# Two key blocks' scores handled as one 2048-wide unit in a decode kernel of attention and a gated mixer

## The chip, the cores and the metric

One core of one Trainium2 chip. The time is device microseconds of one execution; lower is better. Executions of the kernel before agree within 0.2%.

## The reference, cut to what matters

One token attends to 65536 cached keys; 32 query heads share 4 key/value groups. A second branch is a small gated mixer, and a sigmoid gate mixes both.

```python
q = (x @ wq) ...                       # 32 heads of 128
scores = einsum('bhqd,bhkd->bhqk', q, k) * Dh ** -0.5
p = softmax(scores)                    # over 65536 keys
a = einsum('bhqk,bhkd->bhqd', p, v) ... @ wo
b = mixer(x, w_in, w_sp, b_sp, w_out)
out = g * a + (1 - g) * b              # g = sigmoid(sum(x * gate_w))
```

Everything is bf16. The caches are 134 MB of the 162 MB that have to be read, and each byte is used once. Inputs are small (0.05 times normal), so the scores are close to zero.

## The kernel before

The key cache is cut into 16 blocks of 16384 keys ("keys 0" to "keys 15", four per group), 4 MB each, and the value cache likewise. SyncE issues the loads in one fixed order into a ring of five 4 MB slots. Slots 0 to 2 take keys, slots 3 and 4 take values, and most loads are of two blocks, 8 MB. A load is issued only when every block that its slots held has been used up. That is a wait on the last reader: the fourth transpose of a key block on VectorE, or the last value matmul on TensorE.

```python
def k_piece(n, p):                     # a quarter of key block n
    ...
    P("DVE", ... transpose 128x2048 f32 of the quarter into ktb(i) ...)   # two buffers
    if p == 3:
        done(("k", n))                 # the ring slot is free: the next load may be issued
    def f(e): ...                      # 8 score matmuls into sc_ps(n), the half n % 2 of PSUM
    P("PE", f, r=["qpad", ("kt", i % NKT)], w=[KSC(n)])

def score_piece(n):                    # 1024 wide: PSUM -> SBUF, with the running maximum
    P("DVE", lambda e: e.tensor_scalar(scs(n), sc_ps(n), 0.0, None, op0=ALU.add, op1=ALU.max,
                                       accum_out=maxc[:, n:n + 1]), w=[("sc", n % NSC), ("mx", n), KSC(n)])

def exp_piece(n):  ...                 # ScalarE, 1024 wide
def pt_piece(n):   ...                 # VectorE transpose of the probabilities, 1024 wide
def pv_piece(n):   ...                 # TensorE: value matmuls of block n, then done(("v", n))

def k_step(n, evac=None, gmax=None, pts=(), own=False, mid=None):
    for p in range(4):
        k_piece(n, p)
        if p == 0 and evac is not None:
            score_piece(evac)          # evac is n - 1: the other half of PSUM
            ...
```

The load order of the main loop, which the argument needs:

```python
for i in range(6):
    a = 2 * i + 4
    if i % 3 == 2:
        load_k(a, 2)                   # 4 MB each
        load_k(a + 1, 0)
    else:
        load_k2(a, (1, 0)[i % 3])      # 8 MB in one load, needs two free slots
    load_v2(2 * i, VB)
```

## Time and profile before

| | before |
|---|---|
| time, median of 3 (range) | 382.55 us (382.42 to 382.6) |
| bytes read | 162 MB, 425 GB/s over the span |
| load queue, share of 16 engines | 98.6% |
| VectorE / TensorE / ScalarE busy | 55% / 59% / 7% |

From the page of the kernel before: engine shares, then the rows of the span in 40 slices (a digit is the busy share in tenths, PEclk the granted TensorE clock), the load queue, and the chain that ended last.

```profile
PE 223.8 (59%) x1375; PEld 54.6 (14%) x785; DVE 210.4 (55%) x229; ACT 25.4 (7%) x39; POOL 1.8 (0%) x9
DVE  4112596879079606966991069735984990242020
PEclk9997599896869995999896969995899995969766
DMA  9999999999999999999999999999989999999995
q1 hardware_dynamic: 4192, 162.01, 98.6%
DMA 63%; DVE 21%; PE 13%; SPq 1%; issue 0%; ACTq 0%; DVEq 0%
```

The DMA row is 9 nearly everywhere, so the memory stream is the limit and VectorE, with many low digits, is not. But VectorE has 21% of the chain. That is because the chain passes through the transposes that free a ring slot.

The groups of VectorE and ScalarE that the change touches (line, engine, operation, shapes, count; busy us, mean ns of one; idle time of the engine before them, and what ended it):

```profile
L484 DVE STREAM_TRANSPOSE arena<-arena 128x2048 f32<-128x2048 f32 x64 | 145.0, 2290 | 72.0 <-DMA arena<-in_A_k_cache_dram 62.0
L501 DVE TENSOR_SCALAR_CACHE_REDUCE arena<-scp 128x1024 f32<-128x1024 f32 x16 | 19.1, 1191 | 17.6 <-PE scp L248 17.6
L522 DVE STREAM_TRANSPOSE arena<-arena 128x1024 bf16<-128x1024 bf16 x16 | 19.4, 1214 | 8.9 <-PE obt L248 6.4
```

What the change touches is L501 and L522, 38 us in 32 instructions; the 145 us of key transposes stay.

VectorE in order of time in the step of keys 4 (start, duration, engine, line, what):

```profile
106.96 2.31 DVE L484 STREAM_TRANSPOSE arena<-arena 128x2048 f32<-128x2048 f32 x1 [8.70 <-DMA arena<-in_A_k_cache_dram]
109.19 1.19 DVE L501 TENSOR_SCALAR_CACHE_REDUCE arena<-scp 128x1024 f32<-128x1024 f32 x1
...
110.76 2.30 DVE L484 STREAM_TRANSPOSE arena<-arena 128x2048 f32<-128x2048 f32 x1
...
113.23 2.30 DVE L484 STREAM_TRANSPOSE arena<-arena 128x2048 f32<-128x2048 f32 x1
115.46 1.20 DVE L522 STREAM_TRANSPOSE arena<-arena 128x1024 bf16<-128x1024 bf16 x1
116.59 2.27 DVE L484 STREAM_TRANSPOSE arena<-arena 128x2048 f32<-128x2048 f32 x1
```

And the queue of SyncE: the load that this step lets go.

```profile
118.88 0.33 SPq L373 DMA_DIRECT2D arena<-in_A_k_cache_dram  x1
```

The evacuation (L501) follows the first key transpose with no gap. The fourth transpose ends at 118.86, and the load of keys 6,7 is issued at 118.88.

### The profile page before, as it was taken

What the parts mean: (1) busy time and instruction counts of PE and PEld (TensorE: products, weight loads), DVE (VectorE), ACT (ScalarE), POOL (GpSimd) and SP (SyncE); (2) the same over time, 40 slices, a digit from 0 to 9 for tenths busy, and PEclk for the clock granted to TensorE, in tenths of its full rate; (3) what the DMA queues carried; (4) which work ended last, traced back from release to release, by engine and by line L of the source; (5) the groups of instructions that cost most, each with busy time, mean ns of one, the idle gap of its engine ahead of it and who ended that gap; (6) DMA issues with size and microseconds to landing.
All of it is one profiled execution on the core that took longest, in us unless ns stands there. A gap on an engine that the chain in (4) does not pass through costs nothing.

```text
span 381.5 us, 2501 instructions
## 1 busy us (share of the span) xinstructions
PE 223.8 (59%) x1375; PEld 54.6 (14%) x785; DVE 210.4 (55%) x229; ACT 25.4 (7%) x39; POOL 1.8 (0%) x9
## 2 busy tenths in 40 slices
PE   0060479458456844786756636862779643869373
PEld 0010012011011200121111101210112101212031
DVE  4112596879079606966991069735984990242020
ACT  1000000010212000100210001000300100121000
POOL 1000000000000000000000000000000000000000
PEclk9997599896869995999896969995899995969766
DMA  9999999999999999999999999999989999999995
GB/s 440 433 426 405 440 386 436 437 485 443 428 433 405 405 435 440 440 419 436 443 428 440 440 440 440 435 440 434 440 378 414 460 440 433 433 411 429 417 424 212
DMA packets 4238, 162.16 MB, mean 425 GB/s; under 512 B 508, under 2 KB 516, under 8 KB 772
## 3 DMA queue, kind: packets, MB, share of 16 engines
q1 hardware_dynamic: 4192, 162.01, 98.6%
q8 instruction: 8, 0.13, 0.1%
q14 instruction: 2, 0.02, 0.0%
q10 hardware_dynamic: 36, 0.00, 0.0%
HBM read 162.01 MB, written 0.00 MB: 425 GB/s over the span
## 4 chain that ended last, share of the span: by engine, by line
DMA 63%; DVE 21%; PE 13%; SPq 1%; issue 0%; ACTq 0%; DVEq 0%
DMA arena<-in_A_k_cache_dram 40%; DVE arena L484 16%; DMA arena<-in_A_v_cache_dram 10%; DMA arena<-in_A_wo_dram 8%; DMA arena<-in_B_b_sp_dram 5%; PE obt L246 3%; PE obt L248 3%; PE scp L246 3%; PE scp L248 3%; DVE arena L522 2%; DVE arena L501 1%; SPq L373 0%; ACTq L272 0%; SPq L350 0%; PE scp L427 0%
## 5 line engine op out<-in xcount | busy, mean ns | idle before, releaser
L484 DVE STREAM_TRANSPOSE arena<-arena 128x2048 f32<-128x2048 f32 x64 | 145.0, 2290 | 72.0 <-DMA arena<-in_A_k_cache_dram 62.0
L246 PE MATMUL scp<-arena 128*128 128x512 bf16 x256 | 106.3, 415 | 97.5 <-DVE arena L484 94.2
L248 PE MATMUL scp<-arena 128*128 128x512 bf16 x256 | 104.9, 410 | 0.0
L246 PE MATMUL obt<-arena 128*64 128x512 bf16 (+2 forms) x334 | 63.8, 423 | 22.0 <-DMA arena<-in_A_v_cache_dram 22.0
L248 PE MATMUL obt<-arena 128*64 128x512 bf16 (+2 forms) x334 | 63.1, 418 | 0.0
L246 PEld LDWEIGHTS scp<-arena 128*128 128x128 bf16 x256 | 26.2, 103 | 198.7 <-DVE arena L484 124.6
L517 ACT ACTIVATE arena<-arena 128x1024 bf16<-128x1024 f32 x16 | 18.4, 1151 | 226.8 <-DVE arena L522 115.7
L246 PEld LDWEIGHTS obt<-arena 128*64 128x64 bf16 (+1 forms) x334 | 18.6, 114 | 77.6 <-issue 58.8
L501 DVE TENSOR_SCALAR_CACHE_REDUCE arena<-scp 128x1024 f32<-128x1024 f32 x16 | 19.1, 1191 | 17.6 <-PE scp L248 17.6
L522 DVE STREAM_TRANSPOSE arena<-arena 128x1024 bf16<-128x1024 bf16 x16 | 19.4, 1214 | 8.9 <-PE obt L248 6.4
L547 DVE RECIPROCAL arena<-mbt 128x1 f32<-128x1 f32 x4 | 0.7, 168 | 26.3 <-PE mbt L543 26.3
L731 PE MATMUL fbt<-arena 128*1 128x256 bf16 x128 | 6.4, 364 | 4.0 <-DMA arena<-in_A_wo_dram 3.9
L415 PE MATMUL scp<-arena 8*128 8x1 bf16 x8 | 0.6, 197 | 11.1 <-DVE arena L410 11.1
L420 PE MATMUL mbt<-arena 1*128 1x2 bf16 x1 | 0.2, 158 | 10.1 <-DMA arena<-in_B_b_sp_dram 10.1
L737 DVE CAST arena<-fbt 97x256 bf16<-97x256 f32 x1 | 0.4, 425 | 9.7 <-PE fbt L731 9.7
L422 DVE COPY arena<-mbt 128x2 f32<-128x2 f32 x1 | 0.2, 159 | 10.1 <-PE mbt L420 10.1
L562 PE MATMUL mbt<-arena 128*128 128x128 bf16 x16 | 2.0, 262 | 4.7 <-DVE arena L557 4.7
L731 PEld LDWEIGHTS fbt<-arena 128*1 128x1 bf16 x128 | 3.4, 104 | 7.0 <-DMA arena<-in_A_wo_dram 3.0
L606 ACT ACTIVATE arena<-arena 128x28 f32<-128x28 f32 x1 | 0.2, 228 | 56.7 <-DVE arena L605 56.7
L472 DVE COPY arena<-arena 32x32 bf16<-32x32 bf16 x16 | 2.6, 164 | 2.2 <-PE scp L248 2.0
L449 DVE CAST arena<-obt 97x1024 bf16<-97x1024 f32 x1 | 1.2, 1225 | 4.7 <-PE obt L248 4.7
L568 DVE TENSOR_TENSOR arena<-mbt,arena 128x128 f32<-128x128 f32 x4 | 1.2, 292 | 4.4 <-PE mbt L562 4.4
(89 smaller groups left out, 51.0 us busy)
## 6 DMA issues: line engine op xcount, KB each, us to landing
arena<-in_A_k_cache_dram SPq DMA_DIRECT2D x6, 4096.0 KB, 33.5
arena<-in_A_v_cache_dram SPq DMA_DIRECT2D x2, 4096.0 KB, 23.8
arena<-in_B_w_in_dram SPq DMA_DIRECT2D x1, 7168.0 KB, 30.9
arena<-in_A_wo_dram SPq DMA_DIRECT2D x3, 2048.0 KB, 28.6
arena<-in_B_w_out_dram SPq DMA_DIRECT2D x1, 3584.0 KB, 20.7
arena<-in_A_wo_dram SPq DMA_DIRECT2D x1, 1280.0 KB, 30.9
arena<-in_A_wo_dram SPq DMA_DIRECT2D x1, 512.0 KB, 31.6
arena<-in_A_wo_dram SPq DMA_DIRECT2D x1, 256.0 KB, 31.1
```

The source lines that it names most:

```text
L246: return e.matmul(*a, **kw)
L248: one = e.matmul(*a, **kw).ins
L449: P("DVE", lambda e: e.tensor_copy(psb[0:97, :], ob[0:97, :]), w=["psb", "ob"])
L472: P("DVE", lambda e, pb=pb: e.tensor_copy(vw(qpad, 24 + 32 * pb, [[QP, 4], [1, 8]], 32 * pb, 32), vw(qall, 8 * g, [[32, 4], [1, 8]], 32 * ...
L484: P("DVE", lambda e: e.transpose(ktb(i).bitcast(F32), sl[:, 4096 * p:4096 * (p + 1)].bitcast(F32)), r=keys[4 * p:4 * p + 4], w=[("kt", i % ...
L501: P("DVE", lambda e: e.tensor_scalar(scs(n), sc_ps(n), 0.0, None, op0=ALU.add, op1=ALU.max, accum_out=maxc[:, n:n + 1]), w=[("sc", n % NSC ...
L517: P("ACT", lambda e: e.activation(psb, scs(n), ACTF.Exp, bias=gcol(n // NP, K_NB), scale=SCALE, accum_out=lp[:, n:n + 1]), r=[("sc", n % N ...
L522: P("DVE", lambda e: e.transpose(ptsb(n), psb), r=["psb"], w=[("ptsb", n % 2)])
L547: P("DVE", lambda e: e.reciprocal(gcol(g, K_RL), mb[:, 0:1]), w=[("rl", g), "mb"])
L562: ins = e.matmul(mb[:, 0:128], sel[:, 128 * c:128 * (c + 1)], osc[:, 128 * c:128 * (c + 1)], start=(c == 0), stop=(c == 3))
L568: P("DVE", lambda e: e.tensor_tensor(vw(ot, 0, [[8, 16], [1, 8]]), vw(mb, 0, [[8, 16], [1, 8]]), vw(mq, 0, [[1, 16], [0, 8]]), ALU.mult), ...
L731: ins = e.matmul(fb[32 * q:32 * q + 1, 0:QW], ovec[:, 8 * i + c:8 * i + c + 1], sl[:, o:o + QW], start=False, stop=(i == 3 and c == 7), ti ...
```

## The change

Intent: keep the work but halve the number of instructions on VectorE and ScalarE. The scores of two key blocks become one PSUM tile of 2048 columns, evacuated, exponentiated and transposed as one unit; the maximum and the normaliser use fewer small operations; small copies and memsets go to GpSimd. The diff, cut to its core:

```diff
-    scp = [nc.alloc_psum_tensor("scp%d" % i, [128, 1024], F32) for i in range(2)]
+    scp = nc.alloc_psum_tensor("scp", [128, 2048], F32)
...
     def q_piece(g):
         for pb in range(4):
-            P("DVE", lambda e, pb=pb: e.tensor_copy(vw(qpad, ...
+            P("POOL", lambda e, pb=pb: e.tensor_copy(vw(qpad, ...
...
-    def score_piece(n):
-        P("DVE", lambda e: e.tensor_scalar(scs(n), sc_ps(n), 0.0, None, op0=ALU.add, op1=ALU.max,
-                                           accum_out=maxc[:, n:n + 1]), w=[("sc", n % NSC), ("mx", n), KSC(n)])
+    def score_pair(j):
+        P("DVE", lambda e: e.tensor_scalar(scs(j), scp[:, :], 0.0, None, op0=ALU.add, op1=ALU.max,
+                                           accum_out=maxc[:, j:j + 1]),
+          w=[("sc", j % 2), ("mx", j), KSC(0), KSC(1)])
...
-    def k_step(n, evac=None, gmax=None, pts=(), own=False, mid=None):
+    def k_step(n, evac=None, gmax=None, pts=None, mid=None):
         for p in range(4):
             k_piece(n, p)
             if p == 0 and evac is not None:
-                score_piece(evac)
+                score_pair(evac)
...
-            if p == 2 and pts:
-                pt_piece(pts[0])
-                exp_piece(pts[1])
-            if p == 3 and pts:
-                pt_piece(pts[1])
...
+        if pts is not None:
+            pt_pair(pts)
...
-        k_step(a, evac=a - 1, gmax=(a - 1) // NP if a % NP == 0 else None, pts=(2 * i, 2 * i + 1))
+        k_step(a, evac=i + 1, gmax=i // 2 if i % 2 == 0 else None, pts=i)
```

Note the place of `score_pair(evac)`. Before, block n wrote one PSUM half while the evacuation read the other. Now the evacuation reads both halves, and it still stands after the first matmuls of block n. So it waits for them, and those matmuls have already started to overwrite the even block's scores.

More of the change, by code (lines that the diff above doesn't have):

```diff
@@ L166, in bass_gated_mix__gqa_block_cached__mixer_gmlp__decode_kernel @@
     NKT = 2
-    NSC = 5
+    NSC = 4
     QW = DO // 4
@@ L184, in bass_gated_mix__gqa_block_cached__mixer_gmlp__decode_kernel @@
     for name, n in [
-        ("RING", NSUB * SUB), ("KT", NKT * 4096), ("SC", NSC * 2048), ("PSB", 1024), ("PTSB", 2 * 1024),
+        ("RING", NSUB * SUB), ("KT", NKT * 4096), ("SC", NSC * 2048), ("PSB", 2 * 1024), ("PTSB", 2 * 1024),
         ("QPAD", 4 * QP), ("IDB", 128), ("BM", 256), ("SEL", 16 * 32),
         ("M16", 32), ("MQ", 32), ("XT", KC), ("WB", 2), ("WBB", 4), ("ONEB", 128),
-        ("MAXC", 2 * total), ("LP", 2 * total), ("COLS", 2 * 64), ("DM", 32), ("QALL", 128), ("OV", OC), ("MHALF", 4),
+        ("MAXC", 2 * total), ("LP", 2 * total), ("COLS", 2 * 64), ("DM", 64), ("ONES", 256), ("QALL", 128), ("OV", OC), ("MHALF", 4),
         ("YB", FC), ("OROW", QW),
@@ L204, in vw @@
                        ap=[[ps, np_]] + [list(d) for d in dims])
-    idb, bm, ones = ab("IDB", 128), af("BM", 128), af("SC", 128, 4 * 1024 + 896)
+    idb, bm, ones = ab("IDB", 128), af("BM", 128), af("ONES", 128)
     sel, m16, mq = ab("SEL", 512), af("M16", 16), af("MQ", 16)
@@ L212, in bass_gated_mix__gqa_block_cached__mixer_gmlp__decode_kernel @@
     yb, ovec, orow = ab("YB", FC), ab("OV", OC), ab("OROW", QW)
-    dm = af("DM", 16)
-    psb = ab("PSB", 1024)
+    dm = af("DM", 32)
+    psb, psb2 = ab("PSB", 1024), ab("PSB", 2048)
     osc, ot = ab("PSB", 512), af("PSB", 128, 256)
@@ L221, in gcol, with gcol2 @@
         return col(C_G4 + 12 * g + i)
+    def gcol2(g, i):
+        return colt[:, C_G4 + 12 * g + i:C_G4 + 12 * g + i + 2]
     (K_M, K_NB, K_MH, K_L, K_RL, K_F, K_FA, K_FB) = range(8)
     ktb = lambda i: ab("KT", 4096, (i % NKT) * 4096)
-    scs = lambda n: af("SC", 1024, (n % NSC) * 1024)
+    scs = lambda j: af("SC", 2048, (j % 2) * 2048)
     ptsb = lambda i: ab("PTSB", 1024, 1024 * (i % 2))
-    scp = [nc.alloc_psum_tensor("scp%d" % i, [128, 1024], F32) for i in range(2)]
+    ptsb2 = ab("PTSB", 2048)
+    scp = nc.alloc_psum_tensor("scp", [128, 2048], F32)
     obt = nc.alloc_psum_tensor("obt", [128, 1024], F32)
@@ L232, in bass_gated_mix__gqa_block_cached__mixer_gmlp__decode_kernel @@
     fbt = nc.alloc_psum_tensor("fbt", [128, 512], F32)
-    sc_ps = lambda n: scp[n % 2][:, :]
+    sc_ps = lambda n: scp[:, 1024 * (n % 2):1024 * (n % 2 + 1)]
     ob, mb, fb = obt[:, :], mbt[:, :], fbt[:, :]
-    tb = scp[1][:, 0:512]
+    tb = scp[:, 1024:1536]
     tbh = tb.bitcast(BF16)
@@ L249, in mm @@
         return e.add_instruction(dataclasses.replace(one, name=nc.get_next_instruction_name(), ldweights=False))
-    idf = af("SC", 128, 4 * 1024)
-    m8 = af("SC", 8, 4 * 1024 + 128)
-    m32 = af("SC", 32, 4 * 1024 + 136)
-    qT = ab("SC", 32, 4 * 2048 + 400)
+    idf = af("SC", 128, 0)
+    m8 = af("SC", 8, 128)
+    m32 = af("SC", 32, 136)
+    qT = ab("SC", 32, 400)
     P("POOL", lambda e: e.memset(idf, 0.0), w=["idf"])
@@ L261, in bass_gated_mix__gqa_block_cached__mixer_gmlp__decode_kernel @@
     P("POOL", lambda e: e.memset(orow, 0.0), w=["orow"])
-    P("DVE", lambda e: e.memset(ones, 1.0), w=["ones"])
-    P("DVE", lambda e: e.memset(oneb, 1.0), w=["oneb"])
+    P("POOL", lambda e: e.memset(ones, 1.0), w=["ones"])
+    P("POOL", lambda e: e.memset(oneb, 1.0), w=["oneb"])
     P("DVE", lambda e: e.memset(mb, 0.0), w=["mb"])
@@ L272, in f @@
                 return e.dma_start(dst, src)
-        P("ACT", f, w=[key], dma="l%s" % (key if isinstance(key, str) else key[1]))
+        P("ACT", f, w=[key], dma="l" + key)
     xrow, grow, prod = ab("SC", 512, 3 * 2048), ab("SC", 512, 2 * 2048), af("SC", 512, 1 * 1024)
     xm = ab("SC", 1024, 3 * 2048 + 512)
-    KX, KG, KP = ("sc", 3), ("sc", 2), ("sc", 1)
+    KX, KG, KP = "xr", "gr", "pr"
     small(xrow[0:8, 0:128], A_x[0, 0].rearrange("(i n) -> i n", i=8), KX)
@@ L390, in bass_gated_mix__gqa_block_cached__mixer_gmlp__decode_kernel @@
     P("DVE", lambda e: e.tensor_reduce(m16, vw(idf, 0, [[8, 16], [1, 8]]), AXX, ALU.add), r=["idf"], w=["m16"])
-    P("DVE", lambda e: e.tensor_copy(vw(bm, 0, [[8, 16], [1, 8]]), vw(m8, 0, [[0, 16], [1, 8]])), r=["m8"], w=["bm"])
+    P("POOL", lambda e: e.tensor_scalar(m16, m16, -SCALE, None, op0=ALU.mult), r=["m16"], w=["m16"])
+    P("POOL", lambda e: e.tensor_copy(vw(bm, 0, [[8, 16], [1, 8]]), vw(m8, 0, [[0, 16], [1, 8]])), r=["m8"], w=["bm"])
     P("DVE", lambda e: e.tensor_reduce(m32, vw(idf, 0, [[1, 32], [32, 4]]), AXX, ALU.add), r=["idf"], w=["m32"])
-    P("DVE", lambda e: e.tensor_copy(col(C_E4), m32[:, 0:1]), r=["m32"], w=["e4"])
-    P("DVE", lambda e: e.tensor_copy(vw(sel, 0, [[16, 32], [1, 16]]), vw(m32, 0, [[1, 32], [0, 16]])),
+    P("POOL", lambda e: e.tensor_copy(col(C_E4), m32[:, 0:1]), r=["m32"], w=["e4"])
+    P("POOL", lambda e: e.tensor_copy(vw(sel, 0, [[16, 32], [1, 16]]), vw(m32, 0, [[1, 32], [0, 16]])),
       r=["m32"], w=["sel"])
@@ L399, in bass_gated_mix__gqa_block_cached__mixer_gmlp__decode_kernel @@
       r=["idf"], w=["mhalf"])
-    sele = ab("SC", 512, 4 * 2048 + 512)
+    sele = ab("SC", 512, 512)
     KSE = "sele"
     for fe in range(4):
-        P("DVE", lambda e, fe=fe: e.tensor_copy(vw(sele, 128 * fe, [[32, 4], [1, 32]]),
+        P("POOL", lambda e, fe=fe: e.tensor_copy(vw(sele, 128 * fe, [[32, 4], [1, 32]]),
                                                 vw(idb, 64 * (fe // 2) + fe % 2, [[0, 4], [2, 32]])),
@@ L433, in bass_gated_mix__gqa_block_cached__mixer_gmlp__decode_kernel @@
       r=["g"], w=["omg"])
+    P("DVE", lambda e: e.tensor_scalar(mhalf, mhalf, col(C_G), None, op0=ALU.mult), r=["mhalf", "g"], w=["mhalf"])
     wqs, keys = use(("wq", 0))
@@ L471, in q_piece @@
         for pb in range(4):
-            P("DVE", lambda e, pb=pb: e.tensor_copy(vw(qpad, 24 + 32 * pb, [[QP, 4], [1, 8]], 32 * pb, 32),
+            P("POOL", lambda e, pb=pb: e.tensor_copy(vw(qpad, 24 + 32 * pb, [[QP, 4], [1, 8]], 32 * pb, 32),
                                                     vw(qall, 8 * g, [[32, 4], [1, 8]], 32 * pb, 32)),
@@ L504, in max_first @@
     def max_first(g):
-        P("DVE", lambda e: e.tensor_reduce(gcol(g, K_M), maxc[:, NP * g:NP * (g + 1)], AXX, ALU.max),
-          r=[("mx", NP * g + u) for u in range(NP)], w=[("m", g)])
-        P("DVE", lambda e: e.tensor_scalar(dm, m16, gcol(g, K_M), None, op0=ALU.mult), r=["m16", ("m", g)], w=["dm"])
-        P("PE", lambda e: e.matmul(mb[:, 0:16], bm, dm, start=True, stop=True), r=["bm", "dm"], w=["mb"])
+        P("DVE", lambda e: e.tensor_tensor(vw(dm, 0, [[16, 2], [1, 16]]), vw(m16, 0, [[0, 2], [1, 16]]),
+                                           vw(maxc, 2 * g, [[1, 2], [0, 16]]), ALU.mult),
+          r=["m16", ("mx", 2 * g), ("mx", 2 * g + 1)], w=["dm"])
@@ L511, in max_second @@
+        P("PE", lambda e: e.matmul(mb[:, 0:32], bm, dm, start=True, stop=True), r=["bm", "dm"], w=["mb"])
     def max_second(g):
-        P("DVE", lambda e: e.tensor_reduce(gcol(g, K_MH), mb[:, 0:16], AXX, ALU.max), w=[("mh", g), "mb"])
-        P("DVE", lambda e: e.tensor_scalar(gcol(g, K_NB), gcol(g, K_MH), -SCALE, None, op0=ALU.mult),
-          r=[("mh", g)], w=[("nb", g)])
-    def exp_piece(n):
-        P("ACT", lambda e: e.activation(psb, scs(n), ACTF.Exp, bias=gcol(n // NP, K_NB), scale=SCALE,
-                                        accum_out=lp[:, n:n + 1]),
-          r=[("sc", n % NSC), ("nb", n // NP)], w=["psb", ("lp", n)])
@@ L521, in pt_piece, with exp_pair, pt_pair @@
-    def pt_piece(n):
-        P("DVE", lambda e: e.transpose(ptsb(n), psb), r=["psb"], w=[("ptsb", n % 2)])
+        P("DVE", lambda e: e.tensor_reduce(gcol(g, K_NB), mb[:, 0:32], AXX, ALU.min), w=[("nb", g), "mb"])
+    def exp_pair(j):
+        P("ACT", lambda e: e.activation(psb2, scs(j), ACTF.Exp, bias=gcol(j // 2, K_NB), scale=SCALE,
+                                        accum_out=lp[:, j:j + 1]),
+          r=[("sc", j % 2), ("nb", j // 2)], w=["psb", ("lp", j)])
+    def pt_pair(j):
+        P("DVE", lambda e: e.transpose(ptsb2, psb2), r=["psb"], w=[("ptsb", 0), ("ptsb", 1)])
@@ L524, in pv_piece, with pt_half @@
+    def pt_half(n):
+        P("DVE", lambda e: e.transpose(ptsb(n), ab("PSB", 1024, 1024 * (n % 2))), r=["psb"], w=[("ptsb", n % 2)])
     def pv_piece(n):
@@ L540, in out_first, with f @@
     def out_first(g):
-        P("DVE", lambda e: e.tensor_reduce(gcol(g, K_L), lp[:, NP * g:NP * (g + 1)], AXX, ALU.add),
-          r=[("lp", NP * g + u) for u in range(NP)], w=[("l", g)])
-        P("PE", lambda e: e.matmul(mb[:, 0:1], bm, gcol(g, K_L), start=True, stop=True),
-          r=["bm", ("l", g)], w=["mb"])
+        def f(e):
+            for h in range(2):
+                ins = e.matmul(mb[:, 0:1], bm, lp[:, 2 * g + h:2 * g + h + 1], start=(h == 0), stop=(h == 1))
+            return ins
+        P("PE", f, r=["bm", ("lp", 2 * g), ("lp", 2 * g + 1)], w=["mb"])
     def out_second(g):
         P("DVE", lambda e: e.reciprocal(gcol(g, K_RL), mb[:, 0:1]), w=[("rl", g), "mb"])
-        P("DVE", lambda e: e.tensor_scalar(gcol(g, K_F), gcol(g, K_RL), col(C_G), None, op0=ALU.mult),
-          r=[("rl", g), "g"], w=[("f", g)])
-        for h, k in ((0, K_FA), (1, K_FB)):
-            P("DVE", lambda e, h=h, k=k: e.tensor_scalar(gcol(g, k), mhalf[:, h:h + 1], gcol(g, K_F), None, op0=ALU.mult),
-              r=[("f", g), "mhalf"], w=[("fh", g, h)])
+        P("DVE", lambda e: e.tensor_scalar(gcol2(g, K_FA), mhalf, gcol(g, K_RL), None, op0=ALU.mult),
+          r=[("rl", g), "mhalf"], w=[("fh", g)])
     def out_third(g):
         P("DVE", lambda e: e.tensor_scalar(osc, ob[:, 0:512], gcol(g, K_FA), None, op0=ALU.mult),
-          r=[("fh", g, 0)], w=["psb", "ob"])
+          r=[("fh", g)], w=["psb", "ob"])
         P("DVE", lambda e: e.scalar_tensor_tensor(osc, ob[:, 512:1024], gcol(g, K_FB), osc, op0=ALU.mult, op1=ALU.add),
-          r=[("fh", g, 1), "psb"], w=["psb", "ob"])
+          r=[("fh", g), "psb"], w=["psb", "ob"])
         def f(e):
@@ L591, in mixer_piece @@
         NZ = 2 * FB4
-        zr, zt = af("SC", NZ, 3 * 1024), af("SC", NZ, 4 * 1024)
-        KZR, KZT = ("sc", 3), ("sc", 4)
-        zw = lambda i: af("SC", 28, 3 * 1024 + 32 * i)
+        zr, zt = af("SC", NZ, 2 * 1024), af("SC", NZ, 3 * 1024)
+        KZR, KZT = ("sc", 1), "zt"
+        zw = lambda i: af("SC", 28, 2 * 1024 + 32 * i)
         zc = vw(zt, 0, [[32, 28]])
@@ L644, in wout_piece @@
         done(("wout", 0))
-        part = scs(4)
-        P("ACT", lambda e: e.activation(part[0:97, :], ob[0:97, :], ACTF.Copy), w=[("sc", 4), "ob"])
+        part = af("SC", 1024, 2 * 1024)
+        P("ACT", lambda e: e.activation(part[0:97, :], ob[0:97, :], ACTF.Copy), w=[("sc", 1), "ob"])
         def f(e):
@@ L652, in f @@
             return ins
-        P("PE", f, r=["e4", ("sc", 4)], w=["fb"])
-    def k_step(n, evac=None, gmax=None, pts=(), own=False, mid=None):
+        P("PE", f, r=["e4", ("sc", 1)], w=["fb"])
+    def k_step(n, evac=None, gmax=None, pts=None, mid=None):
         for p in range(4):
@@ L665, in k_step @@
                 max_second(gmax)
-            if p == 1 and pts:
-                exp_piece(pts[0])
-            if p == 2 and pts:
-                pt_piece(pts[0])
-                exp_piece(pts[1])
-            if p == 3 and pts:
-                pt_piece(pts[1])
+            if p == 1 and pts is not None:
+                exp_pair(pts)
             if p == 1 and mid is not None:
                 mid()
-        if own:
-            score_piece(n)
+        if pts is not None:
+            pt_pair(pts)
     def out_rest(g):
@@ L683, in bass_gated_mix__gqa_block_cached__mixer_gmlp__decode_kernel @@
     k_step(0)
-    k_step(1, evac=0, own=True)
+    k_step(1)
+    score_pair(0)
     mix = mixer_piece()
@@ L687, in bass_gated_mix__gqa_block_cached__mixer_gmlp__decode_kernel @@
     mixer_rest(*mix)
-    k_step(3, evac=2)
+    k_step(3)
     wout_piece()
@@ L692, in bass_gated_mix__gqa_block_cached__mixer_gmlp__decode_kernel @@
         g = i // 2 if i % 2 == 1 else None
-        k_step(a, evac=a - 1, gmax=(a - 1) // NP if a % NP == 0 else None, pts=(2 * i, 2 * i + 1))
+        k_step(a, evac=i + 1, gmax=i // 2 if i % 2 == 0 else None, pts=i)
         if i == 5:
-            k_step(a + 1, evac=a, own=True, mid=lambda: pv_piece(10))
+            k_step(a + 1, mid=lambda: pv_piece(10))
+            score_pair(7)
             max_first(3)
             max_second(3)
-            exp_piece(12)
+            exp_pair(6)
             pv_piece(11)
             out_first(2)
-            pt_piece(12)
+            pt_pair(6)
             out_rest(2)
@@ L709, in mid @@
                 out_first(g)
-        k_step(a + 1, evac=a, mid=mid)
+        k_step(a + 1, mid=mid)
         if g is not None:
             out_rest(g)
-    exp_piece(13)
-    pt_piece(13)
+    exp_pair(7)
     for n in (12, 13, 14, 15):
@@ L717, in bass_gated_mix__gqa_block_cached__mixer_gmlp__decode_kernel @@
         if n < 14:
-            exp_piece(n + 2)
-            pt_piece(n + 2)
+            pt_half(n + 2)
     out_first(3)
```

## The prediction

> **What bounds the kernel now.** The memory stream. The page's DMA row is 9 in 38 of 40 slices, the load queue takes 98.6% of 16 engines' span, and 162.16 MB move at a mean of 425 GB/s. In the packet records a 64 KB packet takes 2418 ns on one of 16 engines, which is 434 GB/s; the 16 engines together are idle under 0.1 us in each 10 us between 20 and 370 us. The Trainium skill ("DMA: Bandwidth & Descriptors", section Where 436 GB/s comes from) puts the ceiling at 435.2 GB/s, and this trace agrees. VectorE (55%), TensorE (59%) and ScalarE (7%) are not. The chain of waits is 63% DMA; its 21% VectorE is where a transpose frees a ring slot for the next load, early, not late. Issued minus landed bytes at each issue: the queue always held 6.5 us of work or more (6.5 us at keys 4,5; 7.3 us at values 0,1 and keys 6,7; 7.7 us at keys 12,13; 10 to 30 us elsewhere). After the last load (landing near 379 us) come only a matmul, a 0.42 us cast and the store.
>
> **What the change does.** By the slope between the transposes seen (1024 wide 1.21 us, 2048 wide 2.29 us) a pair costs about 2.3 us instead of 2.4 us. Estimates: evacuations save 1.6 us of VectorE in all, probability transposes 1.0, the 16 query copies moved to GpSimd 2.6, set-up copies and memsets 1.7, the small operations of the maximum and the normaliser 3.4. VectorE falls from 210 to about 200 us busy, ScalarE from 25.4 to about 21.5, GpSimd rises from 1.8 to 5 to 9. The skill ("Perfetto Trace Analysis", section Optimizing Scalar/DVE Operations) says grouping helps if the engine is saturated; none is.
>
> It also adds a wait. The evacuation of a pair is recorded after the next even key's first matmuls, and needs both halves of the score tile. So VectorE waits for those 8 matmuls (0.43 us each at the lowered clock, 3.4 us), then evacuates for 2.3 us, instead of at once for 1.2 us. I estimate that ring slots freed by keys 4, 6, 8, 10, 12, 14 come free 3 to 5 us later (keys 6,7 issued near 122.5 instead of 118.9 us) and value slots up to 6 us later. The smallest slack there is 7.3 us: 2 to 4 us are left and the queue stays fed. Delays don't add up: each stage starts when its keys land. (These first matmuls also overwrite the even key's scores before they are read, for pairs 1 to 6. It looks like a fault that the comparison may miss: scores are tiny.)
>
> **On the critical path:** nothing of the savings, nothing of the delays. Predicted 382.5 us, range 381.7 to 383.8. Faster by over 2%: 0.01; within 2%: 0.97; slower by over 2%: 0.02.
>
> **What would show it right.** DMA digits 9 throughout, 98 to 99% for the load queue, the 64 KB packet still at 2418 ns; VectorE about 200 us; a new VectorE wait for score matmuls of 2 to 4 us at pairs 1 to 6; the issue of keys 6,7 3 to 5 us later with its landing unchanged near 145 us.
>
> **What would make it wrong.** A delay above 7.3 us: the queue runs dry and the time grows by the excess. Or slow GpSimd query copies at a group's start, or GpSimd work that slows the packets. A gain needs a shorter start or end; neither is touched.

## The result, and the profile after

| | before | after |
|---|---|---|
| time, median of 6 (range) | 382.58 us (382.39 to 383.05) | 387.08 us (384.56 to 388.25) |
| ratio, 95% interval | | 1.011 (1.0078 to 1.0142) |
| VectorE busy, from the page | 210.4 us | 204.7 us |
| sum of VectorE durations, from the trace | 220.1 us | 209.8 us |

A ratio here is the mean time of one kernel's runs over that of the other's of the same rounds, so it is not quite the ratio of the medians. Executions over 1.5% slower than the fastest of the same kernel are left out of the means. The change is slower by 1.1%, outside the predicted range (381.7 to 383.8), and its runs spread over almost 4 us. The profiled execution is its fastest, 384.56 us.

The page of the changed kernel, the lines that answer to those above:

```profile
PE 240.8 (63%) x1383; PEld 57.3 (15%) x793; DVE 204.7 (53%) x162; ACT 22.2 (6%) x23; POOL 7.5 (2%) x35
DVE  3111597777048813894589028943794688242020
PEclk9996599696857897589969966997589988867776
DMA  9999999999999899999999999899999999999995
q1 hardware_dynamic: 4192, 162.01, 98.5%
DMA 48%; PE 28%; DVE 21%; issue 1%; ACTq 0%; SPq 0%; DVEq 0%
```

VectorE and ScalarE are less busy, as intended. The DMA row still looks full, but it has an 8 in the 14th and the 26th slice, the stages of keys 6,7 and of keys 12,13. (One such digit proves little: the kernel before has an 8 too, in its 30th slice, and its packet records show no idle engine there. The packets have to be looked at.) TensorE has risen from 13% to 28% of the chain.

```profile
L490 DVE STREAM_TRANSPOSE arena<-arena 128x2048 f32<-128x2048 f32 x64 | 145.0, 2292 | 70.6 <-DMA arena<-in_A_k_cache_dram 47.0
L507 DVE TENSOR_SCALAR_CACHE_REDUCE arena<-scp 128x2048 f32<-128x2048 f32 x8 | 18.3, 2292 | 25.5 <-PE scp L252 25.5
L527 DVE STREAM_TRANSPOSE arena<-arena 128x2048 bf16<-128x2048 bf16 x7 | 15.9, 2275 | 6.3 <-PE obt L252 6.3
```

The evacuations now wait 25.5 us for score matmuls. Seen in the waits of VectorE (total us, times, longest), the two lines of the changed kernel are:

```profile
DVE arena L507 <- PE scp L252: 25.5, 8, 4.8
DVE arena L490 <- PE scp L252: 23.6, 18, 6.2
```

In the kernel before, the same two waits were:

```profile
DVE arena L501 <- PE scp L248: 17.6, 2, 15.6
DVE arena L484 <- PE scp L248: 10.0, 5, 6.6
```

Of its 17.6 us, 15.6 are one wait near the end. VectorE, and SyncE's queue, in the step of keys 4 of the changed kernel:

```profile
106.69 2.31 DVE L490 STREAM_TRANSPOSE arena<-arena 128x2048 f32<-128x2048 f32 x1 [10.47 <-DMA arena<-in_A_k_cache_dram]
112.76 2.29 DVE L507 TENSOR_SCALAR_CACHE_REDUCE arena<-scp 128x2048 f32<-128x2048 f32 x1 [3.76 <-PE scp L252]
...
115.20 2.30 DVE L490 STREAM_TRANSPOSE arena<-arena 128x2048 f32<-128x2048 f32 x1
...
117.51 2.29 DVE L490 STREAM_TRANSPOSE arena<-arena 128x2048 f32<-128x2048 f32 x1
120.91 2.31 DVE L490 STREAM_TRANSPOSE arena<-arena 128x2048 f32<-128x2048 f32 x1 [1.11 <-PE scp L252]
123.15 2.27 DVE L527 STREAM_TRANSPOSE arena<-arena 128x2048 bf16<-128x2048 bf16 x1
```

```profile
123.25 0.33 SPq L377 DMA_DIRECT2D arena<-in_A_k_cache_dram  x1
```

VectorE stands still for 3.76 us before the evacuation and for 1.11 us before the fourth transpose, and the load of keys 6,7 is issued at 123.25 instead of 118.88, 4.4 us later. The second wait goes with something else, visible on TensorE in the same step: while VectorE evacuates, TensorE has nothing to do, and its next batch of eight matmuls then starts about 0.43 us apart instead of the 0.22 us of the kernel before. First the changed kernel:

```profile
117.56 0.61 PE L250 MATMUL scp<-arena 128*128 128x512 bf16 x1 [1.59 <-DVE arena L490]
117.97 0.63 PE L252 MATMUL scp<-arena 128*128 128x512 bf16 x1
```

The batch that answers to it in the kernel before:

```profile
113.13 0.39 PE L246 MATMUL scp<-arena 128*128 128x512 bf16 x1 [0.31 <-DVE arena L512]
113.36 0.38 PE L248 MATMUL scp<-arena 128*128 128x512 bf16 x1
```

The Trainium skill ("TensorE: Matmul & The Clock Gate", Part 1: The HAM clock gate) says that the array's clock falls to half after an idle window and rises again after a busy one. The start-to-start times here, 0.43 and 0.22 us, agree with a factor of two, and so does the granted clock: it was 0.50 up to 120.5 us in the changed kernel and 1.00 from 112.3 us on in the kernel before. That the idle stretch kept the clock down is read from these two traces, not tested.

**What the late issue did.** The packet records show when the 16 engines of the queue were fed. A steady 64 KB packet takes 2.42 us. In the changed kernel the engines run out one by one from 123.87 on, and by 124.13 ten of them are idle. The first packet of the new load starts at 124.23, 0.98 us after its issue, and most of the first packets take 2.7 to 3.3 us instead of 2.42. By their completion signals, keys 6,7 then land at 146.3 instead of 145.6. The same happens at keys 12,13. If the bytes of each packet are spread evenly over its time, the landed bytes lie less than 0.1 us behind those of the kernel before at 122 us, 0.9 us at 145 us, 1.1 us at 235 us and 2.1 us from 280 us on. Empty engines are only part of this: between 20 and 370 us they amount to 0.7 us (mean of the 16 engines). The rest is slower packets, which count as busy in the queue's share of 98.5%.

I measure the reserve at an issue as bytes issued minus bytes landed, over 433 GB/s, *less the part of each packet in flight that is already done*. At keys 6,7 this is 5.4 us before and 1.1 us after.

### The profile page after: what moved, and what is told of

It reads as the page before. It is cut to its first block, busy times and chain, and to the rows that moved or that the text cites. A ratio compares the mean times of both kernels' runs of the same rounds, so it can differ in the third digit from the quotient of the medians.

```text
span 383.2 us, 2467 instructions
## 1 busy us (share of the span) xinstructions
PE 240.8 (63%) x1383; PEld 57.3 (15%) x793; DVE 204.7 (53%) x162; ACT 22.2 (6%) x23; POOL 7.5 (2%) x35
## 3 DMA queue, kind: packets, MB, share of 16 engines
q1 hardware_dynamic: 4192, 162.01, 98.5%
## 4 chain that ended last, share of the span: by engine, by line
DMA 48%; PE 28%; DVE 21%; issue 1%; ACTq 0%; SPq 0%; DVEq 0%
DMA arena<-in_A_k_cache_dram 36%; DVE arena L490 14%; PE scp L250 9%; PE scp L252 8%; DMA arena<-in_A_wo_dram 7%; DMA arena<-in_B_b_sp_dram 5%; PE obt L250 5%; PE obt L252 5%; DVE arena L507 4%; DVE arena L527 2%; PE fbt L732 1%; ACTq L276 0%; PE mbt L568 0%; DVE arena L513 0%; DVE arena L563 0%
## 5 line engine op out<-in xcount | busy, mean ns | idle before, releaser
L250 PE MATMUL scp<-arena 128*128 128x512 bf16 x256 | 116.6, 456 | 90.1 <-DVE arena L490 90.0
L252 PE MATMUL scp<-arena 128*128 128x512 bf16 x256 | 115.2, 450 | 0.0
L250 PEld LDWEIGHTS scp<-arena 128*128 128x128 bf16 x256 | 28.4, 111 | 205.0 <-issue 111.3
L507 DVE TENSOR_SCALAR_CACHE_REDUCE arena<-scp 128x2048 f32<-128x2048 f32 x8 | 18.3, 2292 | 25.5 <-PE scp L252 25.5
L522 ACT ACTIVATE arena<-arena 128x2048 bf16<-128x2048 f32 x8 | 16.0, 2002 | 228.3 <-DVE arena L519 200.9
L527 DVE STREAM_TRANSPOSE arena<-arena 128x2048 bf16<-128x2048 bf16 x7 | 15.9, 2275 | 6.3 <-PE obt L252 6.3
L516 PE MATMUL mbt<-arena 128*128 128x32 f32 x8 | 2.3, 380 | 10.5 <-DVE arena L513 10.5
L478 POOL COPY arena<-arena 32x32 bf16<-32x32 bf16 x16 | 3.2, 203 | 251.8 <-PE scp L252 225.2
L530 DVE STREAM_TRANSPOSE arena<-arena 128x1024 bf16<-128x1024 bf16 x2 | 2.5, 1245 | 7.4 <-PE obt L252 7.4
L415 DVE TENSOR_TENSOR arena<-arena 8x1024 bf16<-8x1024 bf16 x1 | 1.2, 1211 | 5.2 <-DMA arena<-in_A_x_dram 5.2
```

What stands on the lines that cost most here:

```text
L250: return e.matmul(*a, **kw)
L252: one = e.matmul(*a, **kw).ins
L415: P("DVE", lambda e: e.tensor_tensor(vw(xm, 0, [[128, 8], [1, 128]], 0, 8), vw(xrow, 0, [[0, 8], [1, 128]], 0, 8), vw(idb, 0, [[1, 8], [0, ...
L478: P("POOL", lambda e, pb=pb: e.tensor_copy(vw(qpad, 24 + 32 * pb, [[QP, 4], [1, 8]], 32 * pb, 32), vw(qall, 8 * g, [[32, 4], [1, 8]], 32 * ...
L507: P("DVE", lambda e: e.tensor_scalar(scs(j), scp[:, :], 0.0, None, op0=ALU.add, op1=ALU.max, accum_out=maxc[:, j:j + 1]), w=[("sc", j % 2) ...
L516: P("PE", lambda e: e.matmul(mb[:, 0:32], bm, dm, start=True, stop=True), r=["bm", "dm"], w=["mb"])
```

## The experiments

The theory after the result, "late slots": the wait puts off the release of ring slots until the queue holds too little to bridge the start of the next load. Rival A: the copies on GpSimd cost it. Rival B: units of 2048 are too coarse, in whatever order. Ten kernels were run, all of which the comparison called correct. The reserve is worked out as above; the table has its smallest value from the load of values 0,1 to that of keys 15.

| run | smallest reserve | median us | ratio (95%) |
|---|---|---|---|
| before | 5.4 us | 382.6 | |
| changed, first time | 1.1 us | 387.08 | 1.011 (1.0078 to 1.0142) |
| e1 changed, again | 0.6 us | 385.62 | 1.0087 (1.0073 to 1.01) |
| e2 changed, evacuate first | 4.2 us | 382.36 | 0.9995 (0.9982 to 1.0008) |
| e3 changed, copies on VectorE | 0.2 us | 387.58 | 1.013 (1.0117 to 1.0143) |
| e4 before, plus the wait | 1.3 us | 385.57 | 1.0081 (1.0066 to 1.0095) |
| f1 before, 2.2 us of delay | 3.4 us | 382.61 | 1.0002 (0.9988 to 1.0015) |
| f2 before, 4.4 us of delay | 1.1 us | 386.29 | 1.0116 (1.0076 to 1.0157) |
| f3 before, 6.6 us of delay | 0.0 us | 392.98 | 1.0274 (1.0254 to 1.0293) |
| f4 changed, loads split | 5.0 us | 382.63 | 1.0004 (0.9991 to 1.0016) |
| g2 evacuate first, loads split | 5.0 us | 382.55 | 1.0004 (0.999 to 1.0018) |

The reserve is of the profiled execution, the median of all of them. Every kernel with 3.4 us or more runs at the time of the kernel before, and every one with 1.3 us or less is slower.

The packet records also tell the loss of each stage. For the issues of keys 6,7, keys 10,11 and keys 12,13 in the changed kernel, e1 to e4 and f1 to f3, this is how much the landed bytes fell further behind those of the kernel before, from 4 us before the issue to 12 us after it:

| reserve at the issue | lost by the stream |
|---|---|
| under 0.1 us (3 stages, all of f3) | 2.0 to 3.4 us |
| 0.2 to 0.3 us (2 stages) | 1.9 to 2.2 us |
| 0.6 to 1.1 us (5 stages) | 0.8 to 1.5 us |
| 1.3 to 1.6 us (3 stages) | 0.6 to 1.2 us |
| 1.8 to 2.4 us (2 stages) | 0.2 to 0.8 us |
| 3.0 to 3.4 us (3 stages) | 0.1 to 0.2 us |
| 3.8 us or more (6 stages) | under 0.1 us |

Between 20 and 370 us the engines are idle for 0.01 us or less in every kernel that is not slower, and for 0.4 to 6.6 us in every one that is.

### e1: the changed kernel again

No edit.

> The changed kernel, once more, for its spread and for a second trace. Both theories: 384.5 to 388.3 us. The late-slot theory also expects this trace to show the load of keys 6,7 and of keys 12,13 issued with under 3 us of work left in the queue, and the landings after them 0.5 to 2 us later than in the kernel before.

Measured: 385.62 us (385.16 to 387.28). Its trace shows 0.6 us of reserve at keys 6,7, 1.5 us at keys 12,13, and landed bytes 1.4 us behind the kernel before after the first and 2.6 us behind after the second.

### e2: the same instructions, without the wait

```diff
-    def k_piece(n, p):
+    def k_piece(n, p, between=None):
...
         if p == 3:
             done(("k", n))
+        if between is not None:
+            between()
         def f(e): ...                                  # the 8 score matmuls
...
-            k_piece(n, p)
-            if p == 0 and evac is not None:
-                score_pair(evac)
+            first = p == 0 and evac is not None
+            k_piece(n, p, between=(lambda: score_pair(evac)) if first else None)
+            if first:
                 if gmax is not None:
```

> The changed kernel with one thing altered: the pair's scores are evacuated before the next even key's first matmuls are issued, so VectorE has nothing to wait for there. VectorE's order of instructions is the same. Late-slot theory (the wait makes ring slots free too late): 382.3 to 383.3 us, keys 6,7 issued near 120 us with 4 us or more of work left in the queue. Rival A (the copies on GpSimd cost it): still 386 to 388 us. Rival B (2048-wide units are too coarse, whatever their order): 385 us or more.

Measured: 382.36 us, no different from the kernel before. VectorE does the same instructions in the same order, but the evacuation follows the first transpose at once:

```profile
106.83 2.31 DVE L490 STREAM_TRANSPOSE arena<-arena 128x2048 f32<-128x2048 f32 x1 [10.02 <-DMA arena<-in_A_k_cache_dram]
109.06 2.25 DVE L509 TENSOR_SCALAR_CACHE_REDUCE arena<-scp 128x2048 f32<-128x2048 f32 x1
...
119.58 0.33 SPq L377 DMA_DIRECT2D arena<-in_A_k_cache_dram  x1
```

(The last line is from SyncE's queue of the same run.) The load of keys 6,7 goes out at 119.58, 0.7 us after the kernel before. Rival B falls: 2048-wide units are as fast as 1024-wide ones here. Rival A falls too, as the copies on GpSimd are all still there. This order also evacuates the scores before they are overwritten, so it is the one to keep of the changed design.

### e3: the copies back on VectorE

```diff
-    P("POOL", lambda e: e.memset(ones, 1.0), w=["ones"])
+    P("DVE", lambda e: e.memset(ones, 1.0), w=["ones"])
...                                                     (likewise oneb, m16, bm, e4, sel, sele)
-            P("POOL", lambda e, pb=pb: e.tensor_copy(vw(qpad, ...
+            P("DVE", lambda e, pb=pb: e.tensor_copy(vw(qpad, ...
```

> The changed kernel with all copies, memsets and the scaling that it gave to GpSimd put back on VectorE. Late-slot theory and rival B: 386 to 388 us, as the changed kernel. Rival A: 382.5 us.

Measured: 387.58 us, as slow as the changed kernel. Rival A falls a second time. This trace caught an execution in which a third stage ran dry as well: the load of keys 10,11 was issued at 203.15, with 0.2 us in reserve; in the first trace of the changed kernel it went out at 199.71, with 3.2 us.

### e4: the kernel before with the wait alone

```diff
-    def score_piece(n):
+    def score_piece(n, wait=()):
...
-                                           accum_out=maxc[:, n:n + 1]), w=[("sc", n % NSC), ("mx", n), KSC(n)])
+                                           accum_out=maxc[:, n:n + 1]), r=list(wait),
+          w=[("sc", n % NSC), ("mx", n), KSC(n)])
...
-                score_piece(evac)
+                score_piece(evac, [KSC(n)] if n >= 4 and n % 2 == 0 else ())
```

> The kernel before, 1024-wide, with the wait alone added: at each even key from 4 on, the evacuation of the key before also waits for the even key's first matmuls. Late-slot theory: keys 6,7 issued 3 to 4 us later than in the kernel before, 3.5 to 4.5 us of work left in the queue, so 382.5 to 384.5 us: most or all of the loss is missing because the slot comes about 1 us earlier than in the changed kernel. Rivals A and B: 382.5 us exactly.

Measured: 385.57 us. The wait alone, on 1024-wide units, costs as much as the whole change did in its second measurement. My expectation (382.5 to 384.5 us) was a miss in size: I had still counted packets in flight as whole, and took 3.5 to 4.5 us for enough where only 1.6 us were left. On VectorE:

```profile
112.96 1.23 DVE L501 TENSOR_SCALAR_CACHE_REDUCE arena<-scp 128x1024 f32<-128x1024 f32 x1 [3.69 <-PE scp L248]
...
122.71 0.33 SPq L373 DMA_DIRECT2D arena<-in_A_k_cache_dram  x1
```

(The last line is again SyncE's queue.) The load went out 3.8 us later than in the kernel before.

### f1, f2, f3: lateness without any wait

The kernel before, with spare reductions on VectorE in each even step. Nothing waits for them except what comes later on VectorE.

```diff
+        if p == 0 and n >= 4 and n % 2 == 0:
+            for x in range(M):                          # M = 1, 2, 3
+                P("DVE", lambda e, x=x: e.tensor_reduce(colt2[:, M * n + x:M * n + x + 1], sl[:, 0:2048], AXX, ALU.max),
+                  r=keys[0:2], w=[("spare", n, x)])
         if p == 3:
             done(("k", n))
```

> The kernel before, with one spare VectorE reduction of 2048 elements (about 2.2 us) put after the first key transpose of each even key from 4 on; nothing else waits. Late-slot theory: ring slots free 2 to 2.5 us later, keys 6,7 issued with about 5 us in the queue, which is enough: 382.3 to 382.8 us.

> The same with two spare reductions (about 4.4 us). The count of landed bytes moves in steps of one 64 KB packet per engine, 2.4 us; so a queue that shows 2.4 us is on its last packet on each engine, and a new load's first packet starts 1.0 us after its issue. Late-slot theory: keys 6,7 issued with 2.4 to 3 us shown, engines idle a little, first packets of the new load above 2.6 us: 383.5 to 386.5 us, as the changed kernel. A theory in which the wait for matmuls matters for another reason than lateness expects 382.6 us.

> The same with three spare reductions (about 6.6 us). Late-slot theory: under 1 us left at keys 6,7 and keys 12,13; each of these stages loses 2 us or more: 387 to 394 us.

Measured: 382.61, 386.29 (383.69 to 388.44) and 392.98 us. The load of keys 6,7 went out at 120.91, 123.21 and 125.45 (one line from SyncE's queue of each run, in this order):

```profile
120.91 0.33 SPq L374 DMA_DIRECT2D arena<-in_A_k_cache_dram  x1
123.21 0.33 SPq L374 DMA_DIRECT2D arena<-in_A_k_cache_dram  x1
125.45 0.33 SPq L374 DMA_DIRECT2D arena<-in_A_k_cache_dram  x1
```

So 2 us of lateness cost nothing, 4 us cost what the changed kernel cost and spread its runs as widely, and 6.6 us cost 10 us. This needs no wait for a matmul and no change of width. In f3 the dry stages can be seen on the page, in the rows of the DMA:

```profile
PE 233.1 (59%) x1375; PEld 55.6 (14%) x785; DVE 250.2 (64%) x247; ACT 25.3 (6%) x39; POOL 1.8 (0%) x9
DMA  9999999999998999899979999899999999999994
GB/s 428 428 428 427 427 417 428 422 487 427 422 427 341 421 429 427 377 428 478 421 334 389 454 434 427 327 422 428 427 417 434 439 427 401 434 407 433 411 425 165
```

The slices of 341, 334 and 327 GB/s, with an 8, a 7 and an 8, are the stages of keys 6,7, of keys 10,11 and of keys 12,13. (The 8 over 377 GB/s is another slice without an idle engine.) In the packet records the first packets of keys 6,7 start 0.97 us after the issue, and most take 3.0 to 3.5 us.

### f4: the wait kept, the reserve given back

```diff
-            load_k2(a, (1, 0)[i % 3])
+            load_k(a, (1, 0)[i % 3])
+            load_k(a + 1, (1, 0)[i % 3] + 1)
```

Each 8 MB load needed two slots, one of which had been free for long. As two loads, the first half goes out early.

> The changed kernel, its wait and its wrong order kept, but each 8 MB key load of the main loop issued as two of 4 MB, one per ring slot, so that its first half needs only the slot of the earlier, long finished key and can be issued early. Late-slot theory: 9 us more work in the queue when the late slot comes free, no idle engines: 382.2 to 383.2 us although VectorE waits as before. If the wait cost time otherwise than through late issues: 385 us or more.

Measured: 382.63 us, the time of the kernel before, though the evacuations still wait for score matmuls:

```profile
DVE arena L508 <- PE scp L252: 29.4, 8, 11.7
```

The longest of these is the last one, which the changed kernel has too (4.8 us). At the six evacuations of the main loop VectorE waits 15.7 us in all, against 18.7 us in the changed kernel (4.01 against 3.76 us at keys 4). SyncE issues keys 6 at 100.22 and keys 7 at 114.20, where the changed kernel issued both at 123.25:

```profile
99.84 0.33 SPq L378 DMA_DIRECT2D arena<-in_A_v_cache_dram  x1
100.22 14.32 SPq L378 DMA_DIRECT2D arena<-in_A_k_cache_dram  x2
```

(The second line merges both issues.) The edit did a second thing: each half now lands by itself, keys 4 at 97.1 us instead of 106.7 us with keys 5, so VectorE began the step earlier, and that is why keys 7 could go out 9 us earlier. The issue had 19.9 us in reserve; 9.05 us later, at 123.25, it would still have had about 10.8 us (an estimate from these two numbers), so the early first half alone was enough. So the wait on VectorE cost nothing by itself. It cost time only through the late issue.

### g1 and g2: what the comparison sees, and both mends together

g1 is wrong: all scores are multiplied by zero.

```diff
-        P("DVE", lambda e: e.tensor_scalar(gcol(g, K_NB), gcol(g, K_MH), -SCALE, None, op0=ALU.mult),
+        P("DVE", lambda e: e.tensor_scalar(gcol(g, K_NB), gcol(g, K_MH), 0.0, None, op0=ALU.mult),
...
-        P("ACT", lambda e: e.activation(psb, scs(n), ACTF.Exp, bias=gcol(n // NP, K_NB), scale=SCALE,
+        P("ACT", lambda e: e.activation(psb, scs(n), ACTF.Exp, bias=gcol(n // NP, K_NB), scale=0.0,
```

> Wrong on purpose: the kernel before with the scores multiplied by zero in the exponential and in the maximum, so that every key gets the same weight. No theory of time is tested. If the comparison calls this correct, it cannot see the overwritten scores of the changed kernel either; if it calls it wrong, the changed kernel's scores must be better than I read. I expect it to be called correct, at 382.5 us.

It was called correct, in one run of 382.58 us. So the comparison with these inputs cannot see scores at all, and "correct" says nothing on the overwritten scores of the changed kernel. That these are wrong for the even block of pairs 1 to 6 is read from the code, not measured.

g2 joins the edits of e2 and f4.

> The changed kernel with both mends: evacuation first (right order, no wait) and the 8 MB key loads split in two. The late-slot theory expects ample work in the queue at every issue (over 10 us at each key load) and no gain beyond the stream: 382.2 to 382.8 us. Any gain over 1 us would say that the queue was short even in the kernel before.

Measured: 382.55 us. More reserve than enough buys nothing. No version tried beats the kernel before by more than the interval.

## Why the prediction was right or wrong

- **"What bounds the kernel now: the memory stream" was right.** Taking 10.4 us of durations off VectorE gained nothing (e2), and adding 13 us in f1 (busy 223.7 us instead of 210.4) cost nothing.
- **The costing of instructions was right as durations, and off as busy time.** I summed 10.3 us of savings on VectorE; the durations fell from 220.1 to 209.8 us, 10.3 us. But busy time fell by 5.7 us only, because neighbouring instructions overlap in the trace, so that removing one does not remove its whole duration. GpSimd rose to 7.5 us, inside the estimate.
- **The new wait was right.** 3.76 us at keys 4 (predicted 2 to 4 us), and the issue of keys 6,7 moved by 4.4 us (predicted 3 to 5 us). But its landing moved by 0.7 us, where I had said it would not.
- **The step that failed: "The smallest slack there is 7.3 us: 2 to 4 us are left and the queue stays fed."** The term was mis-sized twice. I counted only packets that had ended as landed, so each packet in flight counted as whole. One such packet on each engine is 2.4 us; without its finished part the slack was 5.4 us, not 7.3. And I let the reserve go to zero before any loss, while a load's first packet starts 0.98 us after its issue and the first packets run at 2.7 to 3.3 us. The runs put the limit between 1.3 us (e4, slower) and 3.4 us (f1, not slower); stage by stage the loss sets in gradually, with 0.2 to 0.8 us lost at 1.8 to 2.4 us of reserve. So 4.4 us of lateness, which left 1.1 us, was already too much. The signs that I had named could not tell: the queue's share was 98.5% and the median 64 KB packet took 2.418 us, as predicted.
- **"Delays don't add up: each stage starts when its keys land" also failed.** Keys 6,7 were issued 4.4 us late but keys 10,11 were issued 9.4 us late (199.71 against 190.31). Keys 8 had landed at 175.4 in the changed kernel (completion signal), but VectorE came to them only at 184.6 (178.4 before), held up by the step before it. Those stages follow the previous stage, not the landing.
- **What stays open.** The runs of the changed kernel spread over 4 us. Part of it is whether a third stage runs dry: keys 10,11 had 3.2 us of reserve in an execution with a span of 383.2 us and 0.2 us in one (of e3) of 386.2 us. But the second trace of the changed kernel had 2.4 us there and a span of 386.0 us, so this does not explain all. In that trace the landed bytes were 3.1 us behind the kernel before at 375 us and 4.4 us behind at 378 us: the last 1.3 us were lost as the last loads ended unevenly (from 6 to 4 us before the last packet 5.3 engines were busy on average, against 12.8 in the kernel before). Why one execution comes later than another was not tested.

## What to carry to other kernels

In a kernel bound by a stream, ask of each load how much work the queue still holds when it is issued, subtract the finished part of the packets in flight and the microsecond that a new load takes to start, and hold every lengthened wait against what is left. If that is small, let a load need one buffer rather than two, and land by itself (f4), or move a consumer ahead of the producer that would block it (e2); either was enough here. And when two halves of a double buffer are merged into one unit, check who writes the first half before the unit has been read, with inputs for which the comparison can tell.

## What the Trainium skill lacked or had wrong

- "Perfetto Trace Analysis", section What "DMA-bound" means, names which resource binds but not how much lateness a bound queue forgives. Here the DMA row read 9 almost everywhere, with 98.5% occupancy, in a kernel that lost 1.1% to a late feed, and the reserve at each issue told it: 3.4 us or more at every issue was harmless, 1.3 us or less at one was not.
- "DMA: Bandwidth & Descriptors", section Latency and other measured facts, gives about 600 ns to the first byte of such a load without saying from when. Here the first packet started 0.98 us after the start of the issue instruction, 0.65 us after its end. That most first packets of such a late load are slow as well (2.7 to 3.5 us for 64 KB instead of 2.42) is on none of the pages I read.
- "SBUF — State Buffer", in its summary, advises about 358 GB/s for estimating a transfer between HBM and SBUF. One core alone moved 425 GB/s over the whole span here, and 434 GB/s in steady packets; "DMA: Bandwidth & Descriptors", section Bandwidth, already has 425 GB/s for 16 MB in its table of single-core measurements.
